# Fourier layer and cosine-gated MLP on one core: combination's sums moved to VectorE, and a first batch whose Fourier work is handed out more thinly

## The chip, the cores and the metric

The kernel runs on one core of a Trainium2 chip. The metric is the device time of one execution in microseconds, as the median of several runs; smaller is better. The engines are named as in the profile: PE (TensorE, with PEld for its weight loads), DVE (VectorE), ACT (ScalarE), POOL (GpSimd) and SP (SyncE, which issues most DMAs).

## The reference

```python
def attn(x, w_r, w_i, b_r, b_i):          # x: 8 x 3008 x 256, f32
    X = np.fft.rfft(x, axis=1)
    Yr = X.real @ w_r - X.imag @ w_i + b_r
    Yi = X.real @ w_i + X.imag @ w_r + b_i
    # soft threshold of both at lam = 0.01
    Yr = np.sign(Yr) * np.maximum(np.abs(Yr) - lam, 0.0)
    Yi = np.sign(Yi) * np.maximum(np.abs(Yi) - lam, 0.0)
    return np.fft.irfft(Yr + 1j * Yi, n=3008, axis=1)

def moe(x, w_in, w_out):                  # 24064 tokens, 256 -> 2048 -> 256
    h = x @ w_in
    return (h * np.cos(h)) @ w_out

reference = moe(attn(x, ...).reshape(8 * 3008, 256), ...)
```

## The kernel before

**Work and order.** 3008 = 64 x 47, so each Fourier transform is two stages of small matrix products. A batch passes through these steps: stage A (`pa`, over 64 points; `burst` of one or two tiles, with the folds `xe` and `xt` on POOL ahead of it, L448 and L449), its result stored to a scratch in DRAM (L453) and loaded again; stage B forward (`pb`, then the transposes L569 on DVE, again over DRAM); `combine` (L587 to L612), which splits the loaded parts `z` for the mix: rounded copies `Xh` on ACT (L592, L600, L607), their rests `Xl` on DVE (L326, called through `rest`), the sum of the two parts on POOL (L599) and that sum's own rest on POOL (L323, `rest_pool`); `wmix` (`pw`, L658 to L660: three products instead of four, which is why the sum is needed); the threshold on DVE (L669 to L684); a fold on POOL (L697 to L709, `odd` is its last piece) and transposes `tr` on DVE (L714, L715), again over DRAM; the inverse over 47 points (`pi`, with `bo` on ACT and DVE, L735 to L738); and stage C (`pc`, L881), which ends the inverse and makes the MLP's input `xTh` and `xTl`. Products are made in two or three passes of rounded parts, hence the many pairs `h` and `l`. Four groups `q` make up a batch's mix.

**The MLP.** It works on six tiles `t` of 512 tokens a batch (the last of 448) and 16 blocks `f` of the hidden width. A step (b, t, f) is six matmuls `ph` (L919 to L921), then ACT L928, DVE L929 (`u`), ACT L931 (the sine), DVE L932 (the product), ACT L934 (`gh`), the rest `gl` on POOL for two of four `f` and on DVE for the others, and, three steps later, six matmuls `po` (L901 to L905). A place in the program is told below by the number of steps begun up to there, over all batches (96 a batch).

**Hand-out.** The Fourier work of the next batch is a generator, `fourier(b)`, which `ahead(b)` wraps and which `pull` calls twice in each MLP step. Every piece yields a cost; `pull` adds a rate per call to a budget and takes pieces while the budget is positive. The rate follows from `share(b)`, which sums the costs of a batch's pieces, and for the first batch `HEAD`, in which `START` and `FIRST` (L49) stand: pauses of the first batch's Fourier work that `fourier` yields (L816, L821). `BT_WAIT` (L47) is the pause of `stage_c` between its loads `bt` (L872) and its first matmul. A scheduler then sets the final order on each engine from the order in which instructions are written and from what they wait for. `floor()` (L315) adds such a condition: nothing inside it is issued ahead of an earlier MLP step's `gh`, `gl` and product, at present the step before the latest.

**The first batch.** Its own Fourier work stands alone at the start, when the weights are still loaded and split (L267 to L274 and L326, on ACT and DVE). Between its pieces lie three filler tiles, c = 0 to 2, of stage A of batch 1 (`alone`, L501, through `burst_of`). Tiles 1 and 2 are put into `held`, and `release` (L461) stores them behind the first matmuls `pc`; tile 0 is stored at once (L487 to L490).

Of the kernel before, what the change touches and what calls it, by code (L numbers as in the profile page):

```python
# [19 lines left out]
ALU = mybir.AluOpType  # L20
# [25 lines left out]
QUIET, READ, BURST, LAST = 3.0, 1.1, 2.5, 21.0  # L46
BT_WAIT, BT_REST = 8.0, 2.0  # L47
SPREAD, SPREAD_FIRST = 1.15, 0.7
START, FIRST = 12.0, 36.0  # L49


class Hold(float):
# [124 lines left out]
def tile_body(ctx: ExitStack, tc, x, w_r, w_i, b_r, b_i, w_in, w_out,  # L177
              c_fq, c_sig, c_f3, c_ff, c_if, c_iw, c_sgn, out):
    nc = tc.nc
# [132 lines left out]
    mm = nc.tensor.matmul  # L312
    steps = []

    def floor():  # L315

        ctx = ExitStack()
        for ins in steps[-2] if len(steps) > 1 else ():
            ctx.enter_context(tc.issue_after(ins.ins))
        return ctx  # L320

# [8 lines left out]
    def fps(name):  # L330
        if len(ring) >= BANKS:
            assert ring[-BANKS][1]
        p = ps.tile([128, 512], F32, tag="f", name=name, bufs=BANKS)
        if "pro" not in pool:
            ring.append((p, []))
        return p
# [9 lines left out]
    def behind(ins, other, why):  # L346

        tc.add_manual_dep(ins.ins, other.name, mybir.DependencyInfo(
            mybir.DependencyClass.Sync, mybir.DependencyReason.DATA), reason=why)

    def some(name, m):

        if "pro" not in pool:
            return [fps(name) for _ in range(m)]
        p = [ps.tile([128, 512], F32, tag=f"o{h}", name=name, bufs=1) for h in range(2)]
        side.extend((q, []) for q in p)
        return p
# [20 lines left out]
    def stage_out(name):  # L378
        return wk.tile([128, 1024], F32, tag="ao", name=name, bufs=3)
# [52 lines left out]
    def stage_a(b):  # L432
        scr1[b] = dr.tile([2, 24, 32, 2, 256], F32, tag="scr1", name=f"scr1_{b}")
        ld, ev = {}, {}

        def load(c):
            if c < 6:
                ld[c] = wk.tile([128, 2, 2, 256], F32, tag="xt", name="xt", bufs=2)
                with tc.issue_after(mark["f0", 2].ins) if b == 1 else ExitStack():
                    ins = (nc.sync if b == 1 else nc.gpsimd).dma_start(  # L440
                        ld[c].rearrange("p i g d -> p (i g d)"), x[b, :, 1024 * c:1024 * (c + 1)])
                if b == 2 and c < 2:
                    behind(ins, mark["pc"].ins, "first tile")

        def fold(c):
            ev[c] = wk.tile([128, 2, 256], F32, tag="xe", name="xe", bufs=2)
            lo, hi = ld[c][:, :, 0], ld[c][:, :, 1]
            nc.gpsimd.tensor_tensor(out=ev[c], in0=lo, in1=hi, op=ALU.add)  # L448
            nc.gpsimd.tensor_tensor(out=lo, in0=lo, in1=hi, op=ALU.subtract)  # L449

        def store(c, ao, after=None):
            for v in range(2):
                ins = nc.sync.dma_start(  # L453
                    scr1[b][v, 4 * c:4 * c + 4].rearrange("i s r d -> (s r) i d"),
                    ao[64 * v:64 * v + 64].rearrange("p (i d) -> p i d", i=4))
                if after is not None:
                    behind(ins, after.ins, "first tile")

        held = []

        def release():  # L461
            for c, ao in held:
                store(c, ao, mark["pc"])

        def burst_of(cs):
            pro = "pro" in pool
            ps2 = [fps("pa") for _ in range(2)] if pro and cs[0] % 2 else some("pa", 2 * len(cs))
            p = {(c, h): ps2[2 * (c - cs[0]) + h] for c in cs for h in range(2)}
            if b == 1:
                ins = burst(2 - cs[0] % 2 if pro else 2, [((p[c, h][64 * v:64 * v + 64], (ws["minus"] if v * g else ff[:, 256:])[64 * h:64 * h + 64],  # L470
                            ld[c][64 * h:64 * h + 64, :, g]),
                           dict(start=g == 0, stop=g == 1, skip_group_check=True))
                          for c in cs for g in range(2) for h in range(2) for v in (1, 0)])
                if pro:
                    mark["fill"] = mark["pa"] = ins
            else:
                burst(len(ps2), [((p[c, h][64 * v:64 * v + 64], ff[64 * h:64 * h + 64, 256:320],
                                   (ld[c][64 * h:64 * h + 64, :, 0] if v else ev[c][64 * h:64 * h + 64])),
                                  dict(start=True, stop=True, skip_group_check=True))
                                 for c in cs for h in range(2) for v in (1, 0)])  # L480
            for c in cs:
                ao = stage_out("ao")
                for h in range(2):
                    drained(p[c, h], nc.scalar.copy(ao[:, 512 * h:512 * h + 512], p[c, h]))
                    if h == 0 or c < cs[-1]:
                        yield Hold(READ)
                if pro and c:  # L487
                    held.append((c, ao))
                else:
                    store(c, ao)  # L490
                if b > 1:
                    del ld[c], ev[c]
                    load(c + 2)
            yield BURST

        def folds(j):
            for c in (2 * j, 2 * j + 1):
                fold(c)
                yield 0.5

        def alone():  # L501
            load(0)
            load(1)
            yield 0.0
            for tag in ("Xh", "Xl"):
                t = wk.tile([128, 2304], F32, tag=tag, name="x1", bufs=1)
                for k in range(2):
                    c = len(ld)
                    ld[c] = t[:, 1024 * k:1024 * k + 1024].rearrange("p (i g d) -> p i g d", i=2, g=2)
                    nc.sync.dma_start(t[:, 1024 * k:1024 * k + 1024], x[b, :, 1024 * c:1024 * (c + 1)])  # L510
            for c in range(3):
                yield from burst_of([c])

        def begin():
            load(0)
            load(1)

        return SimpleNamespace(begin=begin, folds=folds, alone=alone, release=release, one=lambda c: burst_of([c]),
                               group=lambda j: burst_of([2 * j, 2 * j + 1]))


    def stage_b(b):
# [58 lines left out]
        def combine(q):  # L581

            z = Z.pop(q).rearrange("p (v z g m k) -> p g v z m k", v=2, z=2, g=2, m=8)[..., :24]
            xyh = wk.tile([128, 2304], F32R, tag="Xh", name="Xh", bufs=1)
            xyl = wk.tile([128, 2304], F32R, tag="Xl", name="Xl", bufs=1)
            hi, lo = ([m[:, 768 * r:768 * r + 768].rearrange("p (v m z k) -> p v z m k", v=2, m=8, z=2) for r in range(3)]
                      for m in (xyh, xyl))  # L587
            X[q] = tuple([[m[:, 768 * r:768 * r + 768].rearrange("p (v c x) -> p c v x", v=2, c=2)[:, c] for c in range(2)]
                          for r in range(3)] for m in (xyh, xyl))
            for v in range(2):  # L590
                with floor():
                    nc.scalar.copy(hi[0][:, v], z[:, 0, v])  # L592
                yield 0.8
                with floor():
                    rest(lo[0][:, v], z[:, 0, v], hi[0][:, v])
                yield 0.9
            for v in range(2):
                with floor():
                    nc.gpsimd.tensor_tensor(out=z[:, 0, v], in0=z[:, 0, v], in1=z[:, 1, v], op=ALU.add)  # L599
                    nc.scalar.copy(hi[1][:, v], z[:, 1, v])  # L600
                yield 0.9
                with floor():
                    rest(lo[1][:, v], z[:, 1, v], hi[1][:, v])
                yield 1.2
            for v in range(2):
                with floor():
                    nc.scalar.copy(hi[2][:, v], z[:, 0, v])  # L607
                yield 0.8
                with floor():
                    rest_pool(lo[2][:, v], z[:, 0, v], hi[2][:, v])  # L610
                yield 0.9
# [249 lines left out]
    def stage_c(b, t):  # L861
# [6 lines left out]
        for h in range(0, 4, 2 if first else 4):  # L868
            m = 2 if first else 4
            for g in range(2):  # L870
                n0 = 24 * g + 4 * t + h
                ((nc.scalar, nc.gpsimd)[g] if first else nc.sync).dma_start(  # L872
                    bt[64 * g:64 * g + 64, h:h + m], scr2[b][n0:n0 + m].rearrange("i r s d -> (r s) i d"))
        yield BT_WAIT
        for hf in range(2):
            p = fps("pc")
            with tc.issue_after(mark["pa"].ins) if b == 0 and t == 0 else floor() if b == 0 and t == 1 else ExitStack():
                for j in range(2):
                    for c in range(2):
                        o = 256 * j + 128 * c  # L880
                        ins = mm(p[:, o:o + 128], bt[:, 2 * hf + j, 128 * c:128 * c + 128], ff[:, 128:256], start=o == 0, stop=o == 384,  # L881
                                 skip_group_check=True)
# [110 lines left out]
    for _ in stage_c(0, 0):  # L993
        pass
# [44 lines left out]
    for b in range(NB):  # L1039
        fa = ahead(b)  # L1040
        for t in range(NTT):
# [17 lines left out]
            while open_[0]:  # L1059
                c = next(fa, None)  # L1060
# [30 lines left out]
```

## Time and profile before

| | |
|---|---|
| Median of 3 runs | 2640.63 us (2640.57 to 2641.7) |
| The profiled execution | 2643.39 us, its span 2641.6 us |
| Mean granted clock of PE | 0.995 |
| PE busy | 2603.2 us, 99% of the span |
| DVE, ACT, POOL busy | 73%, 62%, 37% |
| DMA | 282.82 MB, 106 GB/s of HBM traffic over the span |

The trace comes from one profiled execution, and all its times count from the start of its span. What lies outside the span is 2643.39 − 2641.6 = 1.8 us. PE is busy nearly throughout, so a stretch is read by PE's idle time in it and by the granted clock: a stall of the other engines matters only where PE then waits.

### The profile page before, as it was taken

How to read it: one execution, taken by the hardware profiler on the slowest of the kernel's cores; microseconds unless marked ns; L12 is line 12 of the kernel's file. 1: busy time of each engine (PE TensorE's matmuls, PEld its weight loads, DVE VectorE, ACT ScalarE, POOL GpSimd, SP SyncE). 2: the span in 40 equal slices, each digit the busy share in tenths (PEclk: the TensorE clock that was granted, in tenths of full speed). 3: DMA queues.
4: the chain of work that ended last, by engine and by line, in shares of the span. 5: the costliest groups of instructions: out<-in, count | busy, mean ns of one | idle time of the engine just before them, and what ended most of it. 6: DMA issues, size and time to landing. Idle time of an engine off the chain costs nothing.

```text
span 2641.6 us, 38292 instructions
## 1 busy us (share of the span) xinstructions
PE 2603.2 (99%) x13657; PEld 2112.5 (80%) x13657; DVE 1937.9 (73%) x3089; ACT 1635.1 (62%) x3003; POOL 979.1 (37%) x946
## 2 busy tenths in 40 slices
PE   9899999999999999999999999999999999999999
PEld 7478778877788777887788877887778888888888
DVE  5797677878768777687776777677776778766665
ACT  5565556666666666656666666666666666566665
POOL 1224442444425453244533455234432433322222
PEclk9999999999999999999999999999999999999999
DMA  6535434344333444244433544235433343210000
GB/s 209 186 94 150 131 116 129 97 139 137 103 88 107 140 128 116 79 125 137 140 86 86 156 140 116 85 98 143 131 99 101 86 115 108 59 46 17 17 25 16
DMA packets 172935, 282.82 MB, mean 107 GB/s; under 512 B 15608, under 2 KB 114200, under 8 KB 169160
## 3 DMA queue, kind: packets, MB, share of 16 engines
q1 hardware_dynamic: 161896, 243.78, 32.8%
q0 software_dynamic: 10112, 35.53, 4.3%
q8 instruction: 108, 1.77, 0.3%
q10 hardware_dynamic: 736, 1.05, 0.1%
q14 instruction: 83, 0.68, 0.1%
HBM read 149.76 MB, written 130.55 MB: 106 GB/s over the span
## 4 chain that ended last, share of the span: by engine, by line
PE 88%; DVE 7%; ACT 2%; DMA 2%; issue 1%; POOL 1%; SPq 0%; ACTq 0%; DVEq 0%; POOLq 0%
PE ph L919 12%; PE po L901 12%; PE po L905 12%; PE po L902 12%; PE ph L920 12%; PE ph L921 12%; PE pc L881 3%; PE pw L658 2%; PE pw L659 2%; PE pw L660 2%; PE pb L375 1%; PE pw L654 1%; DVE u L932 1%; DVE u L929 1%; DVE Xl L326 1%
## 5 line engine op out<-in xcount | busy, mean ns | idle before, releaser
L323 POOL TENSOR_TENSOR gl<-u,gh 128x512 fp32r<-128x512 f32 (+1 forms) x384 | 502.6, 1309 | 1156.2 <-ACT gh L934 983.4
L931 ACT ACTIVATE u<-u 128x512 f32<-128x512 f32 (+1 forms) x768 | 478.6, 623 | 384.9 <-DVE u L929 383.7
L929 DVE SCALAR_TENSOR_TENSOR u<-ph,u 128x512 f32<-128x512 f32 (+1 forms) x768 | 514.5, 672 | 259.0 <-ACT u L928 257.8
L932 DVE TENSOR_TENSOR u<-ph,u 128x512 f32<-128x512 f32 (+1 forms) x768 | 518.1, 675 | 237.4 <-ACT u L931 226.7
L928 ACT ACTIVATE u<-ph 128x512 int32<-128x512 f32 (+1 forms) x768 | 448.0, 585 | 280.7 <-PE ph L921 271.2
L901 PE MATMUL po<-gh,wout 128*128 128x512 f32 (+1 forms) x1536 | 606.8, 395 | 13.3 <-ACT gh L934 13.1
L934 ACT CAST gh<-u 128x512 fp32r<-128x512 f32 (+1 forms) x768 | 467.9, 609 | 244.8 <-DVE u L932 241.1
L919 PE MATMUL ph<-xTh,win 128*128 128x512 f32 (+1 forms) x1536 | 606.7, 395 | 1.1 <-ACT xTh L886 0.7
L902 PE MATMUL po<-gh,wout 128*128 128x512 f32 (+1 forms) x1536 | 602.1, 392 | 0.0
L920 PE MATMUL ph<-xTl,win 128*128 128x512 f32 (+1 forms) x1536 | 597.3, 389 | 0.0
L921 PE MATMUL ph<-xTh,win 128*128 128x512 f32 (+1 forms) x1536 | 596.1, 388 | 0.0
L905 PE MATMUL po<-gl,wout 128*128 128x512 f32 (+1 forms) x1536 | 480.7, 391 | 0.5 <-POOL gl L323 0.5
L919 PEld LDWEIGHTS ph<-xTh,win 128*128 128x128 f32 x1536 | 289.6, 189 | 90.8 <-issue 20.8
L901 PEld LDWEIGHTS po<-gh,wout 128*128 128x128 f32 x1536 | 289.8, 189 | 79.7 <-ACT gh L934 18.6
L326 DVE TENSOR_TENSOR gl<-u,gh 128x512 fp32r<-128x512 f32 (+1 forms) x384 | 295.6, 770 | 66.9 <-ACT gh L934 59.0
L905 PEld LDWEIGHTS po<-gl,wout 128*128 128x128 f32 x1536 | 288.1, 189 | 66.9 <-issue 5.3
L921 PEld LDWEIGHTS ph<-xTh,win 128*128 128x128 f32 x1536 | 289.6, 189 | 57.5
L902 PEld LDWEIGHTS po<-gh,wout 128*128 128x128 f32 x1536 | 289.8, 189 | 54.6
L920 PEld LDWEIGHTS ph<-xTl,win 128*128 128x128 f32 x1536 | 289.8, 189 | 50.7 <-DVE xTl L887 0.4
L658 PE MATMUL pw<-Xh,wf 128*128 128x384 f32 x336 | 114.9, 342 | 2.0 <-ACT Xh L607 1.9
L659 PE MATMUL pw<-Xh,wf 128*128 128x384 f32 x336 | 114.0, 339 | 0.0
L660 PE MATMUL pw<-Xl,wf 128*128 128x384 f32 x336 | 111.8, 338 | 0.0
(121 smaller groups left out, 2468.5 us busy)
## 6 DMA issues: line engine op xcount, KB each, us to landing
scrF<-at SPq DMA_DIRECT2D x28, 1024.0 KB
z<-scrF SPq DMA_DIRECT2D x112, 256.0 KB
scrT<-tr SPq DMA_DIRECT2D x56, 512.0 KB
y<-scrT SPq DMA_DIRECT2D x112, 256.0 KB
bt<-scr SPq DMA_DIRECT2D x94, 256.0 KB
scr<-ao SPq DMA_DIRECT2D x84, 256.0 KB
scr<-bo SPq DMA_DIRECT2D x224, 96.0 KB
out_dram<-ob SPq DMA_DIRECT2D x80, 256.0 KB
```

What stands on the lines that cost most here:

```text
L323: return nc.gpsimd.tensor_tensor(out=lo, in0=x, in1=hi.bitcast(F32), op=ALU.subtract)
L901: mm(po[e][:, :n], wo[0][:, 0, f, es], gh[:, :n], start=f == 0, stop=False)
L902: mm(po[e][:, :n], wo[0][:, 1, f, es], gh[:, :n], start=False, stop=False)
L905: mm(po[e][:, :n], wo[0][:, 0, f, es], gl[:, :n], start=False, stop=f == NFC - 1)
L919: mm(h, win[:, 0, c, fs], th[:, c, :n], start=c == 0, stop=False)
L920: mm(h, win[:, 0, c, fs], tl[:, c, :n], start=False, stop=False)
L921: ins = mm(h, win[:, 1, c, fs], th[:, c, :n], start=False, stop=c == 1)
L928: nc.scalar.activation(k[:, :n], h, AF.Identity, bias=0.25, scale=1.0 / TWO_PI)
L929: nc.vector.scalar_tensor_tensor(out=u[:, :n], in0=h, scalar=1.0 / TWO_PI, in1=k[:, :n], op0=ALU.mult, op1=ALU.subtract)
L931: nc.scalar.activation(u[:, :n], u[:, :n], AF.Sin, bias=HALF_PI, scale=TWO_PI)
L932: product = nc.vector.tensor_tensor(out=u[:, :n], in0=h, in1=u[:, :n], op=ALU.mult)
L934: step = [nc.scalar.copy(gh[:, :n], u[:, :n])]
```

## The change

It does five things. The sum in `combine` is made on DVE instead of POOL and is written behind the copy `hi[1]`. In batch 1 the rests on DVE and the sums wait for the latest MLP step instead of the one before (`floor(1)`). `START` and `FIRST` are 6 and 24 instead of 12 and 36, which lowers `share(0)` from 63.2 to 59.85 and the rate of the first batch's tiles from 2.44 to 2.33 per call. The pause of the second stage C, tile 1 of the first batch, becomes 2.5 times as long, 20 instead of 8. And filler tile 0 is held like the others. From L602 on, the numbers of the changed kernel are one higher.

```diff
-START, FIRST = 12.0, 36.0
+START, FIRST = 6.0, 24.0
...
-    def floor():
+    def floor(n=2):
...
-        for ins in steps[-2] if len(steps) > 1 else ():
+        for ins in steps[-n] if len(steps) > 1 else ():
...
-                if pro and c:
+                if pro:
                     held.append((c, ao))
                 else:
                     store(c, ao)
...
-                with floor():
+                with floor(1 if b == 1 else 2):
                     rest(lo[0][:, v], z[:, 0, v], hi[0][:, v])
                 yield 0.9
             for v in range(2):
                 with floor():
-                    nc.gpsimd.tensor_tensor(out=z[:, 0, v], in0=z[:, 0, v], in1=z[:, 1, v], op=ALU.add)
                     nc.scalar.copy(hi[1][:, v], z[:, 1, v])
+                with floor(1 if b == 1 else 2):
+                    nc.vector.tensor_tensor(out=z[:, 0, v], in0=z[:, 0, v], in1=z[:, 1, v], op=ALU.add)
                 yield 0.9
-                with floor():
+                with floor(1 if b == 1 else 2):
                     rest(lo[1][:, v], z[:, 1, v], hi[1][:, v])
...
-        yield BT_WAIT
+        yield 2.5 * BT_WAIT if b == 0 and t == 1 else BT_WAIT
```

Three places show what this does to the order on the engines. The first is PE at the second stage C. Before, five steps of `ph` have been issued when the eight `pc` follow:

```order
L919 MATMUL ph<-xTh,win 128x512
L920 MATMUL ph<-xTl,win 128x512
L921 MATMUL ph<-xTh,win 128x512
L881 MATMUL pc<-ff,bt 128x128 x8
L901 MATMUL po_1195<-gh,wout 128x512
L902 MATMUL po_1195<-gh,wout 128x512
```

In the changed kernel they follow after eight steps:

```order
L920 MATMUL ph<-xTh,win 128x512
L906 MATMUL po_1195<-gl,wout 128x512
L906 MATMUL po_1196<-gl,wout 128x512
L921 MATMUL ph<-xTl,win 128x512
L922 MATMUL ph<-xTh,win 128x512
L882 MATMUL pc<-ff,bt 128x128 x8
L902 MATMUL po_1195<-gh,wout 128x512
```

So three more steps of `ph` stand ahead of the `pc`. The second place is DVE in the first batch's steps 41 to 45, where the first group's transposes `tr` and inverse pieces `bo` meet the rests `Xl` of a combination of batch 1:

```order
L932 TENSOR_TENSOR u<-ph,u 128x512
L715 STREAM_TRANSPOSE tr<-odd 128x256
L737 TENSOR_TENSOR bo<-pi,bo 128x512 x2
L738 TENSOR_TENSOR bo<-pi,bo 128x512 x2
...
L682 TENSOR_SCALAR cl<-st,blo,bhi 128x384
L326 TENSOR_TENSOR Xl<-z,Xh 128x2x8x24
L684 TENSOR_TENSOR st<-st,cl 128x8x48
L326 TENSOR_TENSOR Xl<-z,Xh 128x2x8x24 x2
L929 SCALAR_TENSOR_TENSOR u<-ph,u 128x512
```

In the changed kernel the same `tr` and `bo` stand at step 43, and between them and the rests (steps 45 and 47) stand the threshold and the transposes of the next part:

```order
L716 STREAM_TRANSPOSE tr<-odd 128x256
L738 TENSOR_TENSOR bo<-pi,bo 128x512 x2
L739 TENSOR_TENSOR bo<-pi,bo 128x512 x2
...
L326 TENSOR_TENSOR gl<-u,gh 128x512
L716 STREAM_TRANSPOSE tr<-odd 128x256
L715 STREAM_TRANSPOSE tr<-st 128x256 x2
L930 SCALAR_TENSOR_TENSOR u<-ph,u 128x512
L933 TENSOR_TENSOR u<-ph,u 128x512
L326 TENSOR_TENSOR Xl<-z,Xh 128x2x8x24 x2
...
L601 TENSOR_TENSOR z<-z 128x2x8x24
L326 TENSOR_TENSOR Xl<-z,Xh 128x2x8x24
L601 TENSOR_TENSOR z<-z 128x2x8x24
```

The rests stand two to four steps behind the `bo`, and the sums stand among them. For the second group `tr` and `bo` move from step 57 to 59, and rests (and sums) from step 59 to 64. The third place is DVE at a combination of batch 2 (step 150, at 655 us of the trace before), as all later batches have it. Before:

```order
L932 TENSOR_TENSOR u<-ph,u 128x512
L929 SCALAR_TENSOR_TENSOR u<-ph,u 128x512
L932 TENSOR_TENSOR u<-ph,u 128x512
L326 TENSOR_TENSOR gl<-u,gh 128x512
L326 TENSOR_TENSOR Xl<-z,Xh 128x2x8x24 x3
L932 TENSOR_TENSOR u<-ph,u 128x512
L929 SCALAR_TENSOR_TENSOR u<-ph,u 128x512
```

In the changed kernel:

```order
L933 TENSOR_TENSOR u<-ph,u 128x512
L930 SCALAR_TENSOR_TENSOR u<-ph,u 128x512
L933 TENSOR_TENSOR u<-ph,u 128x512
L326 TENSOR_TENSOR gl<-u,gh 128x512
L326 TENSOR_TENSOR Xl<-z,Xh 128x2x8x24
L601 TENSOR_TENSOR z<-z 128x2x8x24
L326 TENSOR_TENSOR Xl<-z,Xh 128x2x8x24 x2
L933 TENSOR_TENSOR u<-ph,u 128x512
L601 TENSOR_TENSOR z<-z 128x2x8x24
```

One sum now stands ahead of the next product, among the three rests, and the other behind it; POOL has two instructions fewer.

## Rows read from the trace of the kernel before

**Rows 1.** The head of the profile's page: the span, busy time of each engine (share of the span) and instructions, and the chain that ended last by engine.

```profile
span 2641.6 us, 38292 instructions
...
PE 2603.2 (99%) x13657; PEld 2112.5 (80%) x13657; DVE 1937.9 (73%) x3089; ACT 1635.1 (62%) x3003; POOL 979.1 (37%) x946
...
PE 88%; DVE 7%; ACT 2%; DMA 2%; issue 1%; POOL 1%; SPq 0%; ACTq 0%; DVEq 0%; POOLq 0%
```

**Rows 2.** The waits of PE over the whole span: waiting line, what it waited for, us in total, times, and the longest in us.

```profile
PE po L901 <- ACT gh L934: 13.1, 8, 4.8
...
PE pc L881 <- DMA bt<-scr: 5.4, 2, 3.6
...
PE pw L658 <- ACT Xh L607: 1.9, 5, 0.4
...
PE pc L881 <- DVE u L932: 1.8, 1, 1.8
...
PE pi L365 <- DMA y<-scrT: 1.3, 1, 1.3
```

**Rows 3.** Stretches of the span: from and to, its length, then busy us (instructions) of PE, PEld, DVE, ACT and POOL, PE's mean granted clock, the DMA share and GB/s.

```profile
120.00:140.00 20.00, 16.42 (x86) 11.18 (x86) 18.11 (x24) 11.09 (x21) 8.75 (x7) 0.91 0.73 238
...
140.00:160.00 20.00, 19.50 (x107) 14.67 (x106) 19.65 (x34) 13.19 (x24) 4.67 (x4) 1.00 0.31 80
...
280.00:296.00 16.00, 11.15 (x38) 8.92 (x38) 13.40 (x21) 8.83 (x18) 9.16 (x8) 0.79 0.34 94
...
345.00:362.00 17.00, 12.77 (x48) 10.26 (x47) 15.69 (x22) 9.92 (x20) 9.43 (x8) 0.80 0.35 102
...
640.00:957.40 317.40, 317.06 (x1698) 258.80 (x1697) 240.37 (x382) 198.82 (x364) 132.40 (x126) 1.00 0.41 116
```

**Rows 4.** PE's instructions in order of time (start in us, duration, instruction, and in brackets the idle time before it and what ended it): those behind the stalls, and two in a row that show the distance from one start to the next.

```profile
131.56 1.13 PE L881 MATMUL pc<-ff,bt 128*128 128x128 f32 x8 [1.75 <-DMA bt<-scr]
...
134.53 1.22 PE L881 MATMUL pc<-ff,bt 128*128 128x128 f32 x4 [1.83 <-DVE u L932]
...
226.82 0.50 PE L901 MATMUL po<-gh,wout 128*128 128x512 f32 x1 [1.15 <-ACT gh L934]
...
227.40 0.40 PE L901 MATMUL po<-gh,wout 128*128 128x512 f32 x1
...
227.63 0.40 PE L902 MATMUL po<-gh,wout 128*128 128x512 f32 x1
...
279.49 0.50 PE L901 MATMUL po<-gh,wout 128*128 128x512 f32 x1 [1.25 <-ACT gh L934]
...
288.76 0.80 PE L901 MATMUL po<-gh,wout 128*128 128x512 f32 x1 [4.85 <-ACT gh L934]
...
354.79 0.80 PE L901 MATMUL po<-gh,wout 128*128 128x512 f32 x1 [4.23 <-ACT gh L934]
...
417.43 0.58 PE L365 MATMUL pi<-y,iw 24*32 24x512 f32 x1 [1.26 <-DMA y<-scrT]
...
658.22 0.45 PE L658 MATMUL pw<-Xh,wf 128*128 128x384 f32 x1 [0.34 <-ACT Xh L607]
```

**Rows 5.** POOL's instructions in order of time at stalls C and D, columns as in group 4.

```profile
260.26 0.55 POOL L440 DMA_DIRECT2D xt<-in_dram  x1 [5.44 <-PE pa L375]
...
266.85 1.59 POOL L448 TENSOR_TENSOR xe<-xt 128x512 f32<-128x512 f32 x1 [4.20 <-DMA xt<-in_dram]
...
273.37 0.59 POOL L707 TENSOR_TENSOR odd<-st 128x184 f32<-128x184 f32 x1
...
281.51 1.41 POOL L323 TENSOR_TENSOR gl<-u,gh 128x512 fp32r<-128x512 f32 x1 [6.29 <-ACT gh L934]
...
283.41 1.25 POOL L599 TENSOR_TENSOR z<-z 128x384 f32<-128x384 f32 x1 [0.49 <-DVE Xl L326]
...
332.43 1.28 POOL L448 TENSOR_TENSOR xe<-xt 128x512 f32<-128x512 f32 x1 [2.28 <-DMA xt<-in_dram]
```

**Rows 6.** DVE's instructions in order of time at stalls C and D, columns as in group 4.

```profile
273.99 0.45 DVE L715 STREAM_TRANSPOSE tr<-odd 128x256 f32<-128x256 f32 x1 [5.90 <-POOL odd L707]
...
281.88 1.45 DVE L326 TENSOR_TENSOR Xl<-z,Xh 128x384 fp32r<-128x384 f32 x1
...
283.72 2.21 DVE L326 TENSOR_TENSOR Xl<-z,Xh 128x384 fp32r<-128x384 f32 x2
...
285.86 0.68 DVE L929 SCALAR_TENSOR_TENSOR u<-ph,u 128x512 f32<-128x512 f32 x1
...
340.62 0.45 DVE L715 STREAM_TRANSPOSE tr<-odd 128x256 f32<-128x256 f32 x1 [2.53 <-POOL odd L707]
...
348.38 1.01 DVE L326 TENSOR_TENSOR Xl<-z,Xh 128x384 fp32r<-128x384 f32 x2
```

**Rows 7.** Instructions grouped by line and shape over the whole span: count, busy us, mean ns of one, and the idle time before them with what ended it.

```profile
L326 DVE TENSOR_TENSOR Xl<-z,Xh 128x384 fp32r<-128x384 f32 x112 | 104.5, 962 | 8.9 <-ACT Xh L592 6.4 <-ACT Xh L600 2.1
...
L599 POOL TENSOR_TENSOR z<-z 128x384 f32<-128x384 f32 x56 | 69.5, 1255 | 24.8 <-DVE Xl L326 24.8
```

**Rows 8.** The steady combination at 655 us, one row each of DVE, POOL and ACT in order of time, columns as in group 4.

```profile
655.72 2.33 DVE L326 TENSOR_TENSOR Xl<-z,Xh 128x384 fp32r<-128x384 f32 x3
...
656.40 1.23 POOL L599 TENSOR_TENSOR z<-z 128x384 f32<-128x384 f32 x1 [3.33 <-DVE Xl L326]
...
657.66 0.51 ACT L607 CAST Xh<-z 128x384 fp32r<-128x384 f32 x1 [0.23 <-POOL z L599]
```

## The prediction

> **What bounds it now.** I start at the busy times and the chain. TensorE (PE) is busy 2603.2 of 2641.6 us, and it holds 88% of the chain that ended last; VectorE (DVE) holds 7% and is busy 73% over the span [rows 1]. So total work on DVE or GpSimd (POOL) is not what counts: a gain can only come out of the 38 us in which PE stands, or out of time in which it runs at a lower clock. The waits of PE say where it stands: 13.1 us on ACT's `gh` in 8 waits (one of 4.8), 5.4 us on `bt` in two loads (one of 3.6), then small ones [rows 2]. The stretches say when. A steady batch (640 to 957.4 us) loses 0.34 us of 317.4 at full clock, so six batches offer almost nothing. The loss lies before 440 us, and in 280 to 296 and 345 to 362 us the granted clock is 0.79 and 0.80 as well [rows 3]. Full clock is the 2.4 GHz level and the lower level is half of it, so 0.79 over 16 us is 6.7 us at half speed, which costs 3.4 us; 0.80 over 17 us costs 3.4 us too. The stalls one by one [rows 4]: A, 131.56 and 134.53 us (1.75 and 1.83 us, second stage C); B, 226.82 (1.15); C, 279.49 and 288.76 (1.25 and 4.85); D, 354.79 (4.23); E, 417.43 (1.26). Only A, C and D are followed by the low level: ahead of it PE had stood 3.6 us (A, in two waits), 6.1 us (C, in two) and 4.23 us (D). After B and E it kept the full level.
>
> **How C and D come about.** At C, POOL issues an `xt` load at 260.26, stands 4.20 us until it lands, folds four tiles, and reaches `odd` at 273.37 [rows 5]. DVE has the transpose of that `odd` next in its queue and stands 5.90 us (273.99) [rows 6]. Behind it sit the four `bo` and the late `u` of the MLP. Just as DVE catches up, the next combination arrives in the same crowd: a rest `Xl` of 1.45 us beside POOL's `gl` at 281.51, two more in 2.21 us beside POOL's sum at 283.41; the MLP's `u` gets its turn at 285.86 only [rows 5, 6]. PE has three steps of lead (12 matmuls of about 0.23 us from start to start, so 2.8 us a step [rows 4]), and they run out. D is the same pattern: a load wait of 2.28 us, DVE idle 2.53 us at 340.62, then rests from 348.38 on. So each stall has two halves, late `odd` and crowded rests.
>
> **What the change does to these.** The sum leaves POOL for DVE, the Fourier work of the first batch comes 2 to 5 MLP steps later, and for batch 1's combinations the rests and sums may come no earlier than one step later. By the order, `tr`/`bo` at C move from step 41 to 43 and the rests from 43 to 45 and 47; at D `tr`/`bo` move from 57 to 59, while the rests go from 59 to 64. The POOL load chain, and with it the late `odd`, stays. What goes is the crowd behind it.
>
> The sum, in us saved, against the profiled execution:
> 1. **C: 8.3.** All of C costs 1.25 + 4.85 + 3.4 = 9.5 [rows 3, 4]. The DVE wait for `odd` remains, so one stall of the small kind stays, at most the 1.25 seen: 9.5 − 1.2 = 8.3. Ends: 3.0 (half the long stall and the low clock stay) and 9.9.
> 2. **D: 7.3.** 4.23 + 3.4 = 7.6; between `bo` and the rests there are now five steps, about 14 us, in place of two, and DVE's delay there was 2.5. I leave 0.3. Ends: 3 and 8.
> 3. **A: 1.5.** The longer pause moves the second stage C from step 5 to 8, 8 us later, so `bt`, which missed by 1.75 us, is there. PE's loss is 1.75 + 1.83 + 1.8 for the clock (0.91 over 20 us [rows 3]) = 5.4. But DVE, which splits the MLP's weights there, is busy 18.11 and 19.65 of 20 us [rows 3]; only its 1.9 + 0.35 of idle can be squeezed, and I take 1.5 of that. Ends: 0 and 5.4.
> 4. **B: 0.9** of 1.15: the rests that crowded before it now come in one group a step later. Ends: −0.5 and 1.15.
> 5. **Held stores: 0.5.** The first `bt` costs PE 3.6 us [rows 2] while stores of filler tiles run; two of these stores now start behind it. The load's own latency stays. Ends: 0 and 3.
> 6. **E: 1.0.** The last transposes run one step later against the inverse, but `bo` of the group before now goes ahead of them. Ends: −3 and 1.3.
> 7. **Sums on DVE: +0.5 over the steady batches.** A sum costs POOL 1255 ns [rows 7]. On DVE no sum stands in the trace; the nearest row is a rest of the same shape, with two inputs too: two in 1.01 us at 348.38, 0.5 each with POOL free, and 1.45 beside POOL [rows 6]. I take 0.55, near the free end, because each sum that leaves POOL also removes the POOL work that held DVE up: rests average 962 ns [rows 7], so much of their time is such waiting. At the steady step three rests take 2.33 us, of which 1.3 falls to the one beside the sum at 656.40, and the copy at 657.66, which waits for that sum, makes `pw` 0.34 us late [rows 4, 8]. After the change: that rest is shorter by 0.8, one sum of 0.55 more stands ahead of the product, and the copy comes earlier. Net about zero to a small gain; ends −3 and +3.
>
> The sum is 8.3 + 7.3 + 1.5 + 0.9 + 0.5 + 1.0 + 0.5 = 20.0 us, so 2643.39 − 20.0 = 2623.4 for the profiled execution. That one lies 2.8 us above the median of the runs, 2640.63; against the median it is 2620.6, and I forecast **2621 us**.
>
> **A rule that speaks against it.** Beside POOL's `gl` a rest took 1.45 us, without POOL 0.5 [rows 5, 6]. The Trainium skill (GPSIMD Engine Reference, Specifications) says that GpSimd shares its interface to SBUF with VectorE and that instructions of VectorE with two inputs in SBUF contend for it; the trace agrees, with these 1.45 against 0.5 us. By that rule a sum that meets a `gl` would cost 1.4, not 0.55, and 56 of them 78 us of DVE in place of 31. The same reference (side-by-side cycle accounting) has GpSimd's elementwise operation 1.96 times as long as VectorE's; an estimate by it is 1255 / 1.96 = 640 ns for a sum, and with it the DVE work would be 36 us.
>
> **Rivals.**
> - *The sums hold up VectorE (slower).* One mechanism: in a steady combination the second product `u` stands behind three rests (2.33 us [rows 8]), and now behind a sum as well; if the sum waits for POOL's `gl`, the `gh` behind it comes too late for its output matmul, in each of the 24 combinations of batches 2 to 7. The price with no slack is two sums, 1.10 us, so 26.4 us; less the 19.5 us of terms 1 to 6 that is +6.9: about 2647.5. It decides from 19.5 / 24 = 0.81 us per combination up. For it: 1.45 us beside POOL. Against: the rest that the POOL sum held gets 0.8 us shorter, and PE idles only 0.34 us per batch now, so the lead is not known to be used up. The shared interface named above is this mechanism. Chance 0.11.
> - *The stalls only move (no change).* The load chain on POOL is untouched; if late `odd` alone makes C and D, these terms are near zero and 20.0 − 15.6 = 4.4 remain: 2636.2. For it: DVE's 5.90 us before the transposes, the largest wait in the crowd. Against: the long stall of PE at C ends at 288.76 with the `gh` of the first product behind the rests, not of one right behind the transposes. Chance 0.12.
> - *Shorter stalls, clock still falls.* A stall of some 3 us is left at C and at D, and the low level follows as it did after 4.23 us. C then saves 9.5 − 3.0 − 3.4 = 3.1 and D 7.6 − 6.4 = 1.2, in place of 15.6 together: 20.0 − 11.3 = 8.7, so 2632. Chance 0.16.
> - The forecast's case has 0.61.
>
> A measurement of this kernel can tell about 0.2%, 5.3 us, from no change. The forecast's case and the third rival lie beyond it on the fast side: faster 0.77. The second lies within it: 0.12. The first lies beyond it on the slow side: 0.11. For the range: the low end is 2612, the forecast with terms 3 and 5 at their upper ends (+3.9 and +2.5) and 2 us of term 7; the high end is 2637, which takes in the second and the third rival; left out are the slow rival and a few hundredths beyond either end.
>
> **What would show it.** In the changed kernel's windows around 280 and 350 us (they come some 4 to 6 us later) the granted clock reads 1.00, and PE's waits on `gh` fall from 13.1 to under 4 us; DVE still shows an idle of several us for `odd` ahead of the first `bo`. The second `pc` shows no idle for `bt`, but DVE stays at 19 of 20 us behind it. DVE's rests fall from 962 ns towards 700, the sums read 0.5 to 0.8 us, and a steady batch takes 317.4 us or a few tenths less. The forecast is wrong if a low-clock stretch stays after 200 us, if a batch takes over 318 us, or if the sums read above 1 us with idle of PE on `gh` behind them.

## The result: slower by 0.6%

The changed kernel takes 2657.61 us (median of 4 runs, 2653.56 to 2660.09), the kernel before 2641.16 beside it: ratio 1.0059, interval 1.0046 to 1.0072. The forecast was 2621, so the sign is wrong. The profiled execution is the shortest of the four, 2653.56 us, 10.2 us above the 2643.39 of before. The other three are 3.2 to 6.5 us longer, and PE's mean granted clock in them is 0.994 instead of 0.996.

The head of the changed kernel's page, and behind it the waits of PE (as in [rows 2]: us in total, times, longest), to be read against [rows 1, 2]; lines are one higher from L602 on:

```profile
span 2651.8 us, 38294 instructions
PE 2605.9 (98%) x13657; PEld 2108.2 (80%) x13657; DVE 1943.0 (73%) x3145; ACT 1636.4 (62%) x3003; POOL 908.9 (34%) x890
```

```profile
PE po L902 <- ACT gh L935: 14.9, 11, 2.2
PE pb L365 <- issue: 5.0, 2, 3.9
PE pi L365 <- DMA y<-scrT: 3.2, 1, 3.2
PE pc L882 <- DMA bt<-scr: 2.6, 1, 2.6
```

POOL has lost 70 us of work and DVE has gained 5: the sums cost 33 us there, but other instructions became shorter. The waits for `gh` are not fewer: no single one of 4.8 us, but eleven of up to 2.2. The stretches show where (columns as in [rows 3]):

```profile
280.00:296.00 16.00, 16.00 (x71) 12.91 (x71) 11.54 (x22) 8.78 (x18) 6.27 (x7) 1.00 0.36 107
...
345.00:362.00 17.00, 17.00 (x85) 14.27 (x84) 16.72 (x28) 11.39 (x22) 5.77 (x5) 1.00 0.54 138
362.00:440.00 78.00, 73.72 (x394) 58.46 (x392) 54.37 (x89) 46.54 (x87) 29.32 (x27) 0.98 0.39 112
...
640.00:957.40 317.40, 314.77 (x1682) 255.40 (x1681) 238.07 (x387) 197.04 (x361) 120.76 (x117) 1.00 0.41 114
```

C and D are gone: PE stands not at all in their stretches, at full clock, and between 195.06 and 418.72 us it has no wait of over 0.7 us. But 362 to 440 us lost 4.3 us where it had lost 1.3, and the steady stretch loses 2.63 us where it lost 0.34. From the first step of batch 1 to the first step of batch 7, the trace of before takes 2361.53 − 463.40 = 1898.1 us, that of the changed kernel 2371.70 − 460.32 = 1911.4: 13.3 us more over six batches, in five of which the Fourier work stands at the same steps as before.

The steady combination, to be read against [rows 8]: the rows of DVE, POOL, ACT and PE, each in order of time.

```profile
652.02 0.54 DVE L326 TENSOR_TENSOR Xl<-z,Xh 128x384 fp32r<-128x384 f32 x1
652.49 0.55 DVE L601 TENSOR_TENSOR z<-z 128x384 f32<-128x384 f32 x1
652.96 2.92 DVE L326 TENSOR_TENSOR Xl<-z,Xh 128x384 fp32r<-128x384 f32 x2
655.80 0.68 DVE L933 TENSOR_TENSOR u<-ph,u 128x512 f32<-128x512 f32 x1
656.40 0.54 DVE L601 TENSOR_TENSOR z<-z 128x384 f32<-128x384 f32 x1
...
652.91 1.29 POOL L323 TENSOR_TENSOR gl<-u,gh 128x512 fp32r<-128x512 f32 x1 [4.53 <-ACT gh L935]
654.15 1.31 POOL L323 TENSOR_TENSOR Xl<-z,Xh 128x384 fp32r<-128x384 f32 x1
...
653.07 0.51 ACT L608 CAST Xh<-z 128x384 fp32r<-128x384 f32 x1 [0.24 <-DVE z L601]
...
657.04 0.51 ACT L608 CAST Xh<-z 128x384 fp32r<-128x384 f32 x1
...
657.18 0.51 PE L902 MATMUL po<-gh,wout 128*128 128x512 f32 x1 [2.20 <-ACT gh L935]
...
658.22 0.34 PE L659 MATMUL pw<-Xh,wf 128*128 128x384 f32 x1
```

And rows of POOL, DVE, ACT and PE in the kernel before at the same place, which follow those of [rows 8]:

```profile
657.58 1.61 POOL L323 TENSOR_TENSOR gl<-u,gh 128x512 fp32r<-128x512 f32 x1
659.16 2.42 POOL L323 TENSOR_TENSOR Xl<-z,Xh 128x384 fp32r<-128x384 f32 x2
...
657.97 0.68 DVE L932 TENSOR_TENSOR u<-ph,u 128x512 f32<-128x512 f32 x1
...
658.68 0.62 ACT L934 CAST gh<-u 128x512 fp32r<-128x512 f32 x1 [0.51 <-DVE u L932]
...
664.71 0.39 PE L901 MATMUL po<-gh,wout 128*128 128x512 f32 x1
```

The sum itself takes 0.55 us, as forecast. The two rests behind it take 2.92 us, because POOL now runs two instructions back to back beside them, its `gl` and then its own rest of the sum. They begin 0.9 and 2.1 us after the first of the three rests (652.02). Before, POOL's sum stood there, waiting for DVE's rest (656.40, [rows 8]); `gl` came behind it at 657.58, 1.9 us after the first rest (655.72), and POOL's rest at 659.16, 3.4 us after it, when DVE was through with its own. The product `u` behind the two rests comes 2.84 us after they begin, `gh` follows, and PE stands 2.20 us.

The late product is only a part of this. In the kernel before, the `po` of the same product starts at 664.71, 5.4 us after its `gh` is made, so with that order a product some 1.5 us later would still have been in time. Two `pw` (the first at 658.22, [rows 4]), twelve `ph` and more `pw` stand ahead of this `po`. In the changed kernel this `po` stands ahead of those `pw` and `ph`, a fourth place where the order differs, which the three shown with the change leave out. The `pw` could not have filled the wait either, since they need the second sum, which on DVE stands behind the product (656.40): its copy on ACT begins 5.0 us after the first rest (657.04), where it began 1.9 us after it before (657.66, [rows 8]). So the move makes two things late, the product and the copy of the second sum, and PE is left without work between them. The same wait of 2.20 to 2.22 us stands in five batches; in one of them the low clock follows. PE's rows there in order of time, and then the stretch behind it:

```profile
1297.73 0.80 PE L902 MATMUL po<-gh,wout 128*128 128x512 f32 x1 [2.21 <-ACT gh L935]
1298.32 0.63 PE L903 MATMUL po<-gh,wout 128*128 128x512 f32 x1
```

```profile
1298.00:1305.00 7.00, 7.00 (x29) 6.04 (x30) 2.76 (x5) 2.85 (x6) 2.68 (x2) 0.81 0.10 20
```

### The profile page after: what moved, and what is told of

Same layout as the page of the kernel before. It is cut to its first block, busy times and chain, and to the rows that moved or that the text cites. A ratio compares the mean times of both kernels' runs of the same rounds, so it can differ in the third digit from the quotient of the medians.

```text
span 2651.8 us, 38294 instructions
## 1 busy us (share of the span) xinstructions
PE 2605.9 (98%) x13657; PEld 2108.2 (80%) x13657; DVE 1943.0 (73%) x3145; ACT 1636.4 (62%) x3003; POOL 908.9 (34%) x890
## 4 chain that ended last, share of the span: by engine, by line
PE 87%; DVE 7%; DMA 2%; ACT 2%; issue 1%; POOL 0%; SPq 0%; ACTq 0%; DVEq 0%; POOLq 0%
PE ph L920 12%; PE po L902 12%; PE po L903 12%; PE ph L921 12%; PE ph L922 12%; PE po L906 12%; PE pc L882 3%; PE pw L659 2%; PE pw L660 2%; PE pw L661 2%; PE pb L375 1%; DVE u L933 1%; PE pw L655 1%; DVE Xl L326 1%; DVE u L930 1%
## 5 line engine op out<-in xcount | busy, mean ns | idle before, releaser
L323 POOL TENSOR_TENSOR gl<-u,gh 128x512 fp32r<-128x512 f32 (+1 forms) x384 | 494.8, 1289 | 1168.3 <-ACT gh L935 958.7
L902 PE MATMUL po<-gh,wout 128*128 128x512 f32 (+1 forms) x1536 | 606.3, 395 | 15.6 <-ACT gh L935 14.9
L326 DVE TENSOR_TENSOR gl<-u,gh 128x512 fp32r<-128x512 f32 (+1 forms) x384 | 285.4, 743 | 61.9 <-ACT gh L935 56.3
L708 POOL TENSOR_TENSOR odd<-st 128x184 f32<-128x184 f32 (+1 forms) x112 | 68.9, 618 | 137.7 <-DVE st L685 106.9
```

Of the source, the lines that this page charges most:

```text
L323: return nc.gpsimd.tensor_tensor(out=lo, in0=x, in1=hi.bitcast(F32), op=ALU.subtract)
L902: mm(po[e][:, :n], wo[0][:, 0, f, es], gh[:, :n], start=f == 0, stop=False)
```

## The experiments

The kernel before, run beside these, took 2642.6 to 2642.9 us; the ratio to it stands with each experiment. The changed kernel was not run beside them, so a difference from it is to be read with its own ratio, 1.0059.

**1. The sum back on POOL.** The changed kernel, with

```diff
+                    nc.gpsimd.tensor_tensor(out=z[:, 0, v], in0=z[:, 0, v], in1=z[:, 1, v], op=ALU.add)
                     nc.scalar.copy(hi[1][:, v], z[:, 1, v])
-                with floor(1 if b == 1 else 2):
-                    nc.vector.tensor_tensor(out=z[:, 0, v], in0=z[:, 0, v], in1=z[:, 1, v], op=ALU.add)
```

> The changed kernel with the sum on POOL again, written ahead of the copy hi[1] as before; the thinner hand-out, the longer pause, the held store and floor(1) of the rests stay. Theory N (neighbours): on DVE the sum ends early, POOL's gl and POOL's own rest Xl then run back to back beside the last two rests of DVE (2.92 us for two, at 652.96 us), and the product behind them is late; then a batch from the third on falls from some 321 to 317.4 us, which is 13 us over the five, and the 4.0 us stall at 191 us goes too: about 2636 us (2630 to 2645). Rival L (load): the sums' own 0.55 us on DVE make it; the same time follows here. Rival H (hand-out): the thinner hand-out makes the loss; then it stays near 2655 us and a batch near 321.

Measured: 2636.82 us (2634.03 to 2640.43), ratio 0.9980, interval 0.9971 to 0.9989. Batches 1 to 6 take 1897.6 us, as before (1898.1). So the sum on DVE costs 2657.6 − 2636.8 = 20.8 us (0.79% by the ratios, the same), and the rest of the change gains 5.8. H falls; N and L are not told apart by this run.

**2. The sum alone on DVE.** The kernel before, with the sum moved as in the change and the old `floor()`.

```diff
-                    nc.gpsimd.tensor_tensor(out=z[:, 0, v], in0=z[:, 0, v], in1=z[:, 1, v], op=ALU.add)
                     nc.scalar.copy(hi[1][:, v], z[:, 1, v])
+                with floor():
+                    nc.vector.tensor_tensor(out=z[:, 0, v], in0=z[:, 0, v], in1=z[:, 1, v], op=ALU.add)
```

> The kernel before with the sum on DVE alone, written behind the copy hi[1], with the old floor. N and L: the five later batches lose their 13 us, and the combinations of the first batch lose something as well: 2653 to 2665 us. H: no change, 2640 us within 3.

Measured: 2659.24 us (2658.37 to 2663.86), ratio 1.0069, interval 1.0054 to 1.0084. The later batches lose 14.4 us of it in its trace, and the waits that make stalls C and D grow (4.85 us to 6.3 at C). Both N and L forecast this. The `po` stands ahead of the `pw` here as in the change, and PE waits 2.20 to 2.21 us in five batches.

**3. POOL's rest on DVE as well.** This and the next tell the sum's own load from its neighbours.

```diff
-                    rest_pool(lo[2][:, v], z[:, 0, v], hi[2][:, v])
+                    rest(lo[2][:, v], z[:, 0, v], hi[2][:, v])
```

> The changed kernel with the sum's own rest (lo[2]) on DVE too, so that POOL has nothing of the combination. N: beside DVE's rests only a gl can run, so two rests take 1.9 instead of 2.92 us, and a batch takes 317.4 to 319: about 2646 us (2641 to 2651). L: DVE has 2 x 0.55 us more at each combination, the stall of 2.2 us grows by about 1 per combination that has no slack, and a batch takes 322 or more: 2662 us (2657 to 2680).

Measured: 2647.36 us (2645.63 to 2652.06), ratio 1.0021, interval 1.0011 to 1.0031. DVE has more to do and the kernel is 10 us faster than the change. L forecast 2662, N 2646; the two rests take 2.12 us, not the 1.9 that N named.

**4. POOL's rest behind those of DVE.** Nothing moves to another engine; POOL's rest only waits.

```diff
-                    rest(lo[1][:, v], z[:, 1, v], hi[1][:, v])
+                    last = rest(lo[1][:, v], z[:, 1, v], hi[1][:, v])
...
-                    rest_pool(lo[2][:, v], z[:, 0, v], hi[2][:, v])
+                    behind(rest_pool(lo[2][:, v], z[:, 0, v], hi[2][:, v]), last.ins, "rests")
```

> The changed kernel in which POOL's rest of the sum waits for the latest rest of DVE (lo[1]) that is written ahead of it; the order on each engine stays. N: the stall of 2.2 us at the combination falls by the 1.3 us of that POOL rest, to below 1 us, and a batch takes 318 to 319.5: about 2648 us (2644 to 2652). L: nothing changes, 2657 us within 3, or a little more where the rest on POOL comes late for its matmul.

Measured: 2645.48 us (2642.60 to 2647.63), ratio 1.0012, interval 1.0002 to 1.0021. An added wait makes the kernel 12 us faster. Rows of DVE, POOL and PE at the same combination, each in order of time:

```profile
650.19 2.13 DVE L326 TENSOR_TENSOR Xl<-z,Xh 128x384 fp32r<-128x384 f32 x2
652.24 0.68 DVE L933 TENSOR_TENSOR u<-ph,u 128x512 f32<-128x512 f32 x1
...
650.15 1.29 POOL L323 TENSOR_TENSOR gl<-u,gh 128x512 fp32r<-128x512 f32 x1 [4.54 <-ACT gh L935]
652.45 0.99 POOL L323 TENSOR_TENSOR Xl<-z,Xh 128x384 fp32r<-128x384 f32 x1 [1.02 <-DVE Xl L326]
...
653.62 0.50 PE L902 MATMUL po<-gh,wout 128*128 128x512 f32 x1 [1.40 <-ACT gh L935]
```

The two rests take 2.13 us in place of 2.92, the wait of PE 1.40 in place of 2.20. In experiment 3 it is 2.12 and 1.41. So a first 0.8 us of the stall is POOL's rest beside those of DVE. N had the time, but not the stall, which it put below 1 us. What is left has several parts. From the first rest to the product it is 2.98 us (649.26 to 652.24) where it is 2.25 in experiment 1 (645.00 to 647.25); of these 0.73 us the sum takes 0.47 from start to start, and the rests beside POOL's `gl` 0.26. Besides, the second sum stands behind the product and the `po` ahead of the `pw`, in experiments 2, 3 and 4 as in the change. No run separates these. N holds for 10 to 12 of the 20.8 us, and L falls as the whole cause; as a part it stays: experiments 3 and 4 are still 9 to 10 us slower than experiment 1.

**5. No floor(1).** From here on the sum is on POOL; every kernel is that of experiment 1 with one more edit. They ask which part of the change took C and D away.

```diff
-                with floor(1 if b == 1 else 2):
+                with floor():
```

> The changed kernel with the sum on POOL (e1_sum_back, 2636.8 us) and without floor(1): the rests of batch 1 come at steps 44, 46, 61 and 64 in place of 45, 47 and 64. Theory P: stalls C and D came from rests that stand right behind the inverse pieces bo, so the distance counts; three rests now stand two steps behind bo at D and stall D returns in part, 2 to 5 us: 2638 to 2642 us. Rival Q: the thinner hand-out alone removed C and D; then 2637 within 2.

Measured: 2639.05 us (2637.29 to 2641.44), ratio 0.9984, interval 0.9975 to 0.9994: 2.2 us above experiment 1, whose interval overlaps with this one. P's figure, but not its place: C comes back as two waits of 1.20 and 1.45 us, with no low clock, and D, which P named, as one of 0.81.

**6. The old hand-out.**

```diff
-START, FIRST = 6.0, 24.0
+START, FIRST = 12.0, 36.0
```

> e1_sum_back with START and FIRST at 12 and 36 again (hand-out as before; floor(1), the pause and the held store stay). By the order, bo stands at steps 41 and 57, rests at 45 and 62, the last inverse pieces at 79 instead of 81. P: rests are four and five steps behind bo, so C and D stay away, and the stall at the last inverse (3.2 us and a clock fall of 3.4 us) goes as well: about 2631 us (2628 to 2635). Q: C and D return, some 15 us: 2645 to 2652.

Measured: 2638.83 us (2636.93 to 2644.02), ratio 0.9988, interval 0.9978 to 0.9997. Neither theory has the time. The last inverse waits 0.81 us, as P had it. But at C, although the rests stand four steps behind `bo`, PE waits three times, and at D twice (2.33 and 1.61 us, at 348.92 and 355.14). The rows of DVE and PE, and then DVE in experiment 1 for comparison:

```profile
271.72 0.45 DVE L715 STREAM_TRANSPOSE tr<-odd 128x256 f32<-128x256 f32 x1 [5.99 <-POOL odd L707]
285.44 2.29 DVE L326 TENSOR_TENSOR Xl<-z,Xh 128x384 fp32r<-128x384 f32 x3
...
277.22 0.50 PE L901 MATMUL po<-gh,wout 128*128 128x512 f32 x1 [1.35 <-ACT gh L934]
284.85 0.79 PE L901 MATMUL po<-gh,wout 128*128 128x512 f32 x1 [3.19 <-ACT gh L934]
289.04 0.50 PE L901 MATMUL po<-gh,wout 128*128 128x512 f32 x1 [1.26 <-ACT gh L934]
```

```profile
273.99 0.45 DVE L715 STREAM_TRANSPOSE tr<-odd 128x256 f32<-128x256 f32 x1 [2.11 <-POOL odd L707]
```

The wait for `odd` is 5.99 us with the old hand-out and 2.11 with the new one. The long stall of PE (284.85) ends before the first rest (285.44) begins, so rests had no part in it. Told by place: from the 33rd to the 65th MLP step, where C and D lie, experiment 1 takes 120.5 us, experiment 5 takes 123.2, this kernel 132.8 and the kernel before 133.0, with about as many matmuls each. From there to the end of the batch it is 107.9, 106.7, 97.7 and 100.5. (Each is counted from ACT's first instruction of the step, L928.) So nearly all that was won at C and D came from the thinner hand-out, as Q had it, and some 2.7 us from floor(1). What Q left out is that with the thinner hand-out the stretch behind, with the last inverse, takes most of it back; so floor(1) left out costs 2.2 us and the hand-out left out only 2.0. At C the thinner hand-out shortens the wait for `odd`. At D that wait is no shorter (3.30 us in experiment 1, 2.57 here, 2.53 before), so what helps there is not shown.

**7. The short pause.**

```diff
-        yield 2.5 * BT_WAIT if b == 0 and t == 1 else BT_WAIT
+        yield BT_WAIT
```

> e1_sum_back with the short pause ahead of the second stage C: pc at step 5 instead of 8, pb at 9 instead of 12. If the longer pause was worth its term of 1.5 us, 2638 us; if it took the whole of stall A away, 2641; if it only moved the work into the stalls at 152 and 190 us, 2633 to 2636. The waits for bt and for the product ahead of pc (1.75 and 1.83 us before) come back in all three.

Measured: 2632.98 us (2630.76 to 2633.81), ratio 0.9960, interval 0.9945 to 0.9975: 3.8 us faster than experiment 1. The longer pause costs time. Two stretches, of experiment 1 and of this run:

```profile
110.00:150.00 40.00, 37.54 (x180) 25.45 (x181) 34.46 (x53) 24.43 (x45) 14.69 (x14) 0.95 0.70 228
150.00:195.00 45.00, 40.26 (x225) 30.57 (x224) 38.69 (x60) 29.59 (x54) 14.79 (x13) 1.00 0.36 96
```

```profile
110.00:150.00 40.00, 34.47 (x191) 22.15 (x193) 33.41 (x51) 22.82 (x41) 15.71 (x16) 0.97 0.73 231
150.00:195.00 45.00, 44.49 (x232) 35.32 (x225) 41.42 (x66) 31.87 (x59) 15.94 (x14) 1.00 0.36 99
```

With the long pause PE stands 4.7 us in 150 to 195 us and with the short one 0.5. In 110 to 150 us it is the other way round, 2.5 against 5.5, so the long pause saves there less than it costs later. These two stretches make 1.2 of the 3.8 us. The two traces as a whole differ by 0.3 us only, since that of experiment 1 is the shortest of its ten runs; from the first MLP step of batch 0 to that of batch 1 they take 342.6 and 338.9 us, and PE stands 12.8 and 10.6 us there. Of the waits ahead of `pc` only that for `bt` comes back, with 0.90 us. The third of the three cases named came out, and a little beyond.

**8. The last inverse later.**

```diff
             yield None
+        if b == 0:
+            yield 9.0
         yield from g
```

> e1_sum_back with a pause of 9 ahead of the last inverse of batch 1: its pieces come at step 83 instead of 81. Theory: the change moved the last wmix (73 to 76) further than the last inverse (79 to 81), so one step less of PE work covers the way of y over DRAM, and PE stands 3.2 us and falls to the low clock; two steps more cover it, and 4 to 6.5 us go: 2631 us (2629 to 2634). Rival: the load of y is held by other transfers and comes later with it; no change, 2637 within 2.

Measured: 2632.41 us (2631.58 to 2636.61), ratio 0.9962, interval 0.9949 to 0.9975: 4.4 us faster than experiment 1. The stretch of the last inverse, of experiment 1 and of this run:

```profile
400.00:440.00 40.00, 36.27 (x213) 29.30 (x212) 25.27 (x44) 22.94 (x44) 8.59 (x8) 0.91 0.40 111
```

```profile
400.00:440.00 40.00, 38.63 (x239) 32.62 (x239) 29.39 (x52) 25.93 (x49) 10.68 (x11) 1.00 0.37 100
```

The wait and the low clock behind it both go; the rival falls.

**9 and 10. What the runs point to, with and without the held store.** Experiment 1 with the edits of 7 and 8; and the same with `if pro and c:`, so that tile 0 is stored at once.

```diff
-                if pro:
+                if pro and c:
                     held.append((c, ao))
```

> The changed kernel with the sum on POOL, the short pause of before ahead of the second stage C and a pause of 9 ahead of the last inverse of batch 1; START and FIRST at 6 and 24, floor(1) and the held store stay. If the gains of f3_no_btwait (3.8 us) and f5_inv_late (4.4 us) lie in different stretches, they add: 2636.8 - 3.8 - 4.4 = 2628.6 us (2626 to 2631). If one of them only shifts what the other removes, 2632 us, as each had alone.

> g1_best with filler tile 0 stored at once, as before. The forecast's term of 0.5 us for the held store: 2629.1 us; nothing: the same as g1_best within 1 us; if the first load of bt was slowed by these stores, up to 3 us slower.

Measured: 2629.65 us (2628.51 to 2630.72), ratio 0.9953, interval 0.9939 to 0.9967; without the held store 2631.53 (2629.58 to 2634.27), ratio 0.9960, interval 0.9947 to 0.9973. The two gains add but for 1 us, and this kernel is faster than both that the case began with. The held store is worth 1.9 us by the medians, but the ranges and the intervals overlap, so this is not clear of the noise. In the traces the first `bt` keeps PE waiting 2.75 us with it and 3.76 without. This holds throughout: 2.58 to 2.96 us in the nine kernels that hold the store, 3.63 to 3.76 in the three that do not, so some 0.9 us is the store's.

## Why the prediction was wrong

**Term 7, the sums: +0.5 forecast, −20 measured.** This is the step that failed, and it alone turns the sign. The sum's own price was right (0.55 forecast; 598 ns mean). Two of its premises were wrong. The first is that each sum leaving POOL takes away the POOL work that held DVE up. POOL was not emptied there, it was moved forward: the sum on POOL had waited for DVE's rest and so had kept POOL's `gl` and POOL's rest behind DVE's rests. Without it both run beside them; experiments 3 and 4 show that POOL's rest there makes 10 to 12 of the 20.8 us. The mean rest of DVE fell from 962 ns to 913 only, not towards 700:

```profile
L326 DVE TENSOR_TENSOR Xl<-z,Xh 128x384 fp32r<-128x384 f32 x112 | 99.8, 913 | 4.6 <-ACT Xh L592 4.4
L601 DVE TENSOR_TENSOR z<-z 128x384 f32<-128x384 f32 x56 | 32.9, 598 | 0.0
L323 POOL TENSOR_TENSOR Xl<-z,Xh 128x384 fp32r<-128x384 f32 x56 | 72.8, 1308 | 69.0 <-ACT Xh L608 67.9 <-PE pc L882 1.0
```

The second premise is that "the copy comes earlier". Only one of the two sums is made among the rests. The other stands behind the product, its copy comes 3.1 us later against the first rest (5.0 us in place of 1.9), and the `pw` with it. The `po` that had 5.4 us of slack before then stands first in PE's order, with none. That the slow copy and this order make the rest of the 20.8 us, with POOL's `gl` and the sum's own time, is argued from the rows; no run tests it.

Of the 19.5 us by which the profiled executions of the change and of experiment 1 differ, some 13.8 lie in the later batches and 5.8 ahead of them. Of the 5.8, 2.5 us lie ahead of the first MLP step (116.47 against 113.99 us), where no sum is made yet, so they are not the sum's. Behind it the same pair of rests takes 2.92 us again (189.17 us), and a `pb` stands 3.86 us and starts at 195.06, as the first of the products that DVE begins at 194.28 is done. In experiment 1 that `pb` stands 0.58 us; in experiments 3 and 4 it still stands 3.53, so POOL's rest is not what makes this wait.

**The slow rival** had the right engine and place, but not the right victim: rests were held, not the sum. Two rests take 1.01 us where POOL is idle as they begin [rows 6], 2.13 beside one instruction of POOL and 2.92 beside two. By the Trainium skill (GPSIMD Engine Reference, Specifications) GpSimd's interface to SBUF is shared with VectorE, and VectorE's instructions with two inputs in SBUF contend for it; the trace agrees, with these three times. The rival spread the price over 24 combinations at 1.10 us; the profile shows one stall of 2.2 us in each of five batches and small ones besides. It was given 0.11, and its 2647.5 us are still 10 short of the measured time.

**Terms 1 and 2, C and D: 15.6.** Right in result: both stretches run at full clock, PE losing 0.2 and 0.4 us in experiment 1. Mostly wrong in cause: the late `odd` at C, said to stay, shrank from 5.90 to 2.11 us, and experiments 5 and 6 show that the thinner hand-out did nearly all of it and the rests' later place some 2.7 us. The rival "the stalls only move" had named the late `odd` at C; it was wrong in that the change leaves it as it is. The price was also counted high by about 1 us, since the low clock at D begins while PE still stands, in the kernel before:

```profile
352.96:354.79 1.83, 0.00 (x0) 0.00 (x0) 1.83 (x5) 1.83 (x5) 0.50 (x1) 0.50 0.00 0
```

These 1.83 us stand in the 4.23 us of the wait, and half of them once more in the 3.4 us for the clock.

**Term 3, the second stage C: +1.5 forecast, −3.8 measured** for the longer pause alone (experiment 7). The cover that failed: the stage's waits went, but PE stood later, between 150 and 195 us. That DVE would take the gain back there was written down; that it would take more was not.

**Term 6, the last inverse: +1.0 forecast.** PE waited 3.17 us instead of 1.26 and fell to the low clock. The last mix moved by three steps and the inverse by two, so one step less covered the way of `y` over DRAM; experiment 8 gets 4.4 us back.

**Term 4** held: no wait is left at B in the changed kernel. **Term 5** was put at 0.5; by the waits for the first `bt` it is about 0.9.

Together: without the sum the change gains 5.8 us by the medians (9.4 by the profiled executions, experiment 1's being its shortest run), where the forecast had 19.5 for terms 1 to 6. Terms 3 and 6 account for some 9 of what is missing: 1.5 + 3.8, and 1.0 + 4.4 − 1.3 for the wait that was there before. The other 4 us or so are not accounted for. The sum's 20.8 then outweighs the gain: −5.8 + 20.8 = +15.0 us, where the change and the kernel before, run side by side, differ by 16.5.

What stays open: how the 9 to 10 us that remain between experiments 3 and 4 and experiment 1 divide between the second sum behind the product with PE's changed order, the sum's own time, and POOL's `gl` beside the rests (a run with both sums ahead of the product would tell); and why the low clock follows the stall of 2.2 us in one batch and not in the four others. In experiment 2, at a mean clock of 0.993, it follows the same stall in three batches of five. More such falls would go with the lower mean clock and the 3.2 to 6.5 us of the other three runs of the change; those runs have no trace, so this is not shown.

## What to carry to other kernels

Before moving an operation off an engine, look at what stands behind it in that engine's queue: an instruction that waits is also a spacer, and without it its followers run earlier, perhaps beside just those instructions of another engine which they slow down. Ask of a tight place not how long the moved operation takes but which instruction follows it on either engine and what then runs at the same time; experiment 4 won 12 us with a wait and nothing else. Ask also what the moved operation now stands behind, and what work the bottleneck loses when its result comes late: here PE had 5.4 us of slack before that `po`, and none after. And when a chain is moved by pieces, compare how many steps each link moved: a producer that moves by three and a consumer by two have lost a step of cover.

## What the runs showed of the hardware that was not expected

Two back-to-back POOL instructions held two two-input rests of DVE for most of their 2.55 us: 2.92 us for what takes 1.01 alone.

The length of a single wait does not tell in these traces whether PE's granted clock falls to the low level behind it. It fell after waits of 3.2 us (`pi` in experiments 1 and 7, 0.91 over 400 to 440 us), of 2.21 us at 1297.73, in three of the five waits of 2.2 us of experiment 2, and after one of 1.40 us in experiment 4 (1929.21; the clock reads 0.50 from 1929.9 to 1933.2 us). It stayed at the full level after four waits of 2.20 to 2.22 us of the changed kernel and after one of 2.86 us in experiment 5 (109.68).
